# A chunked state-space scan feeding a GELU MLP: other queues for the decay rows, weight casts in pieces, and a new order of all steps

## The chip, the cores and the metric

The kernel runs on one core of a Trainium2 chip, in one launch. The metric is device time in microseconds (us) of that core. Five engines work beside one another and meet at semaphores: TensorE (PE, matmuls; its weight loads are shown as PEld), VectorE (DVE), ScalarE (ACT), GpSimd (POOL) and SyncE (SP, which here only issues DMAs). Each engine takes its own instructions strictly in the order in which they were emitted, so one that waits holds back all behind it.

## The reference, cut to what matters

Two stages, the second fed by the first. Stage one is a gated linear recurrence over 768 steps for 4 batches of 8 heads (head size 32, state size 16), written in chunks; stage two is a two-layer MLP with tanh GELU over the 3072 tokens, 256 wide, 2048 hidden.

```python
cum = np.cumsum(log(clip(a, 1e-06, 1.0)) of the chunk)
M = einsum('bhin,bhjn->bhij', C, B) * exp(cum_i - cum_j) * causal
y = M @ x + (C @ state) * exp(cum)
state = exp(sum) * state + sum_j B_j x_j * exp(cum_end - cum_j)
...
h = y.reshape(tokens, 256) @ w_in
out = gelu_tanh(h) @ w_out
```

Inputs and output are float32; the kernel multiplies in bf16.

## The kernel before, in words

The scan is done in chunks of 128 steps, 6 in a batch, 24 in all. A unit is one chunk (units 0 and 1) or two (units 2 to 12). The steps carry these names, in functions `f_<name>`:

- `clip`, `R`, `RT`, `recip` (DVE): suffix products of the decay, transposed, and their reciprocals. `pe`, `pp`, `pend`: the decay of whole chunks, brought to all rows by one matmul. POOL builds the constants that these need: `ident`, `bmask`, `tri`, `m8`; DVE builds `par` from `bmask` and `sel8`, `selp` from `ident`.
- `mul` (DVE): B times the suffix product, C times its reciprocal, one product each for a batch (`bc16`). `T` (PE): six transposes of such a product. `E`: copy of the result out of PSUM (`ch` for C, `bh` for B). `F` (or `F0` for batch 0): two copies of C masked by the parity of the head (`ce`). `N` (PE) and `bn`: B transposed back, and its copy.
- for a unit: `castx` (x to bf16), `G` (PE: C times B, into `gb`), `M` (DVE: the causal mask, `m`), `D` (PE: B times x, into `hp`), `S` and `SP` (DVE: the new state and its spread form), `Y` (PE: the unit's y, into `yb`), `yev` (ACT: y to `xm` in bf16).
- for the MLP: `s1` (PE: x times w_in, groups of four or eight matmuls into `hp` or `o_ps`), `gelu` (ACT, one for each group, into `gT`), `s2` (PE: four quarters of four matmuls for each chunk), `oev` (copy out of PSUM) and `store`. A group of s1 of units 0 and 1 needs one quarter of w_in, and a quarter of s2 one quarter of w_out.

From unit 4 on, `Y` of a unit, `D` and `G` of the next are emitted as one step. The weights come as float32: w_in in two loads of 1 MB (`wf`, each of two quarters), w_out in four of 512 KB, and are cast into `w_in_sb` [128, 2, 2048] and `w_out_sb` [128, 16, 256] on chip; the two "k halves" of a w_in quarter lie 2048 elements apart in a row. The casts, x among them, go through a helper (`copy`), so that they carry its line in the profile (L254 on POOL, L252 on ACT, L256 on DVE).

The order on each engine is not written by hand. Every step is a `Node` with an engine, a planned duration, the nodes that it needs, buffers that it takes from rotating pools, and a priority; `run_order` plays the plan through in time, takes at each moment the ready node with the lowest priority number on the engine that is free first, and emits the steps in that order. Loads are nodes of an engine "DMA", in the order in which they are added. Where TensorE would stand idle before the first `s1`, `idle` puts in filler matmuls on a zero tile `wz` (L747).

Before the plan starts, the decay rows `a` are fetched in four quarters:

```python
for q, eng in enumerate((nc.sync, nc.scalar, nc.scalar, nc.gpsimd)):
```

All other loads and the stores are issued from SP.

Of the kernel before, what the change touches and what calls it, by code (L numbers as in the profile page):

```python
# [14 lines left out]
class Node:  # L15


    def __init__(self, eng, dur, fn, deps=(), prio=0.0, done=0.0):
        self.eng, self.dur, self.fn, self.prio, self.done = eng, dur, fn, prio, done
        self.deps = [d for d in deps if d is not None]  # L20
        self.allocs = []
        self.after = 0.0
        self.start = self.end = None
# [7 lines left out]
def run_order(nodes, pools, hop=0.08, same=0.04, idle=None, wait=()):  # L31
# [6 lines left out]
    def est(n):  # L38
# [6 lines left out]
        for pool, _ in n.allocs:  # L45
            h = hist[pool]
            if len(h) >= pools[pool]:
                for d in h[-pools[pool]]:
                    if d.end is None:
                        return None  # L50
                    t = max(t, d.end + (same if d.eng == n.eng else hop))
        return t

    while todo:
# [25 lines left out]
        if idle is not None and eng == "PE":  # L80
            x = idle(free.get(eng, 0.0), t)
            if x is not None:
                order.append((free.get(eng, 0.0), x))
# [5 lines left out]
        order.append((t, n.fn))  # L89
    return order  # L90
# [3 lines left out]
def kernel(  # L94
# [24 lines left out]
    UNITS = [[0], [1]] + [[c, c + 1] for c in range(2, NCH, 2)]  # L119
    NU = len(UNITS)  # L120

# [32 lines left out]
    for q, eng in enumerate((nc.sync, nc.scalar, nc.scalar, nc.gpsimd)):  # L154
# [11 lines left out]
    for q in range(4):  # L166
        for t in (Q - 1, 2 * Q - 1) if q % 2 == 0 else (2 * Q - QS - 1, QS - 1):
# [6 lines left out]
    ident = const.tile([128, 128], BF16, name="ident")  # L174
    make_identity(nc, ident)
# [6 lines left out]
                            compare_op=ALU.is_ge, fill=0.0, base=N - 1, channel_multiplier=-1)  # L182
    tri = const.tile([128, Q], BF16, name="tri")
# [20 lines left out]
    par = const.tile([128, 2], FP32, name="par")  # L204
    bmp = bmask.rearrange("p (g e d) -> p e g d", g=4, e=2)
    for e in range(2):
        nc.vector.tensor_reduce(out=par[:, e:e + 1],
                                in_=bmp[:, e, :, 0:1].rearrange("p g o -> p (g o)"),
                                op=ALU.add, axis=mybir.AxisListType.X)
# [21 lines left out]
    def load_x(u):  # L231
        b, c = divmod(UNITS[u][0], CPB)
        XF[u] = ldx.tile([128, 2, H, D], FP32, name="x_t")
        for k in range(len(UNITS[u])):
            nc.sync.dma_start(out=XF[u][:, k], in_=x[b, :, (c + k) * Q:(c + k + 1) * Q, :]  # L235
                              .rearrange("h p d -> p h d"))

    wi = moe_w_in.rearrange("(k d) f -> d k f", d=128)
    wo = moe_w_out.rearrange("(q p k) m -> q p k m", p=128, k=4)

    def load_wi(h):
        WF[h] = wfp.tile([128, 2, d_ff // 2], FP32, name="wf")
        nc.sync.dma_start(out=WF[h], in_=wi[:, :, h * (d_ff // 2):(h + 1) * (d_ff // 2)])  # L243

    def load_wo(q):
        if q % 2 == 0:
            WF[("o", q // 2)] = wfp.tile([128, 8, d_model], FP32, name="wf")
        nc.sync.dma_start(out=WF[("o", q // 2)][:, 4 * (q % 2):4 * (q % 2) + 4], in_=wo[q])  # L248
# [9 lines left out]
    def f_wi(q, k0, k1, eng):  # L258
        copy(eng, w_in_sb[:, k0:k1, q * 512:(q + 1) * 512],
             WF[q // 2][:, k0:k1, 512 * (q % 2):512 * (q % 2) + 512])  # L260

    def f_wo(q, eng):
        copy(eng, w_out_sb[:, 4 * q:4 * q + 4], WF[("o", q // 2)][:, 4 * (q % 2):4 * (q % 2) + 4])
# [52 lines left out]
    def f_T(b, i):  # L316
        bc = U[b]["bc16"].rearrange("p i r h n -> p i r (h n)")
        if b == 0 and i == 1:
            T6_0[1] = pso.tile([128, 512], FP32, name="o_ps")[:, 0:S // 2].bitcast(BF16)
# [3 lines left out]
    def f_E(b, i, eng, p0=0, p1=128):  # L323
# [7 lines left out]
    def f_F0(e, eng, p0, p1):  # L331
# [27 lines left out]
    def f_bn(b, eng, c0=0, c1=CPB):  # L359
# [87 lines left out]
    def f_yev(u):  # L447
        n = len(UNITS[u])
        t0 = UNITS[u][0] * Q
        nc.scalar.activation(xm[:, :, t0:t0 + n * Q].rearrange("p w (c t) -> p c w t", c=n),  # L450
                             y4[:, 0:n], AF.Copy)
# [71 lines left out]

    MERGE = 4
# [3 lines left out]
    def add(eng, dur, fn, *args, deps=(), prio=0.0, done=None):  # L528
        n = Node(eng, dur, (lambda: fn(*args)), deps, prio,
                 (0.26 if eng == "PE" else 0.0) if done is None else done)  # L530
        n.name = f"{fn.__name__}{args}"
# [4 lines left out]
    TD = 1.85  # L536

    def none():
# [10 lines left out]

    an = load(TD + 0.3, none)  # L550
    an.done = 1.3

    def load_bc_n(b, *which):
        for i in which:
            bl[(b, i)] = load(1.6, load_bc, b, i)

    def load_x_n(*us):
        for u in us:
            xl[u] = load(0.87 * len(UNITS[u]), load_x, u)

    def load_w_n(*qs, o=False):
        for q in qs:
            if o:
                won_l[q] = load(1.5, load_wo, q)
            else:
                win_l[q] = load(2.5, load_wi, q)

    load_bc_n(0, 1, 0)
    load_w_n(0)
    load_x_n(0, 1)  # L570
    load_w_n(1)
    load_x_n(2)
    load_w_n(0, 1, 2, 3, o=True)
    load_x_n(3)
    for b in range(1, batch):
        load_bc_n(b, 1, 0)
        load_x_n(3 * b + 1, 3 * b + 2, 3 * b + 3)
    for q in range(4):
        wi_n[q] = [add(e, d, f_wi, q, k0, k1, e, deps=[win_l[q // 2]], prio=-9 + 0.1 * q)
                   for k0, k1, e, d in (((0, 1, "POOL", 0.53), (1, 2, "ACT", 0.56)) if q == 0 else  # L580
                                        ((0, 2, "POOL", 1.06),))]
        wo_n[q] = add("POOL", 1.06, f_wo, q, "POOL", deps=[won_l[q]], prio=20 + q)
# [201 lines left out]
```

## Time and profile before

| | us |
|---|---|
| median of 4 runs | 122.91 |
| lowest, highest | 122.55, 124.58 |
| the profiled execution's own time | 122.93 |
| its span, first to last instruction | 121.2 |
| TensorE busy | 111.1 (92%) |
| ACT busy | 75.0 (62%) |
| DVE busy | 63.0 (52%) |
| POOL busy | 20.5 (17%) |

A line of the profile names the source line, the engine, the operation, what it writes and reads, the shapes and the count. Busy time of TensorE is time with a matmul in flight, not time at its peak; the row PEclk gives the granted clock in tenths of full speed, the row DMA the mean busy share of the 16 DMA engines, both in 40 slices of the span. The chain of work that ended last follows the program back from its last instruction, at each step to what released it.

### The profile page before, as it was taken

The numbers are of one execution on the slowest core, as the hardware profiler recorded it, in microseconds if no ns is written. First come the engines' busy times: TensorE is split into PE (matmuls) and PEld (weight loads), VectorE is DVE, ScalarE is ACT, GpSimd is POOL, SyncE is SP. The second block draws the span as 40 slices with busy tenths as digits, with TensorE's granted clock in tenths as the row PEclk, the third lists the DMA queues.
The fourth block names the chain that finished last, engine by engine and source line by source line (L and its number), as shares of the span: only waits on it lengthen the run. The fifth ranks groups of instructions, "written<-read, shape, count | busy, mean of one in ns | idle before, by whom it ended". The sixth has DMA issues, their size and how long they took to land.

```text
span 121.2 us, 3425 instructions
## 1 busy us (share of the span) xinstructions
PE 111.1 (92%) x1470; PEld 98.3 (81%) x1470; DVE 63.0 (52%) x113; ACT 75.0 (62%) x145; POOL 20.5 (17%) x38
## 2 busy tenths in 40 slices
PE   4987549999999999999999999999999999999970
PEld 4964437988978888998889979798988999999950
DVE  5697932969539995908598527565563000000110
ACT  4029516695657675586675777775768766876210
POOL 5807086622212511202000000000000000000000
PEclk9999995999999999999999999999999999999998
DMA  2999989998899997811101101101110111101121
GB/s 61 297 334 219 246 265 381 220 231 151 153 289 164 185 275 123 149 47 49 43 0 43 47 2 43 46 3 49 43 43 0 49 43 46 43 6 43 43 87 46
DMA packets 38047, 13.96 MB, mean 115 GB/s; under 512 B 33824, under 2 KB 37008, under 8 KB 38032
## 3 DMA queue, kind: packets, MB, share of 16 engines
q1 hardware_dynamic: 37904, 13.67, 47.6%
q8 instruction: 11, 0.18, 0.7%
q10 hardware_dynamic: 96, 0.06, 0.2%
q14 instruction: 4, 0.03, 0.1%
q0 software_dynamic: 32, 0.02, 0.1%
HBM read 10.60 MB, written 3.15 MB: 113 GB/s over the span
## 4 chain that ended last, share of the span: by engine, by line
PE 66%; SPq 17%; DVE 7%; DMA 5%; issue 1%; DVEq 0%
PE o_ps L508 28%; PE hp L491 27%; SPq L248 6%; DMA bc_t<-in_B_dram 5%; SPq L243 4%; SPq L151 4%; SPq L235 3%; PE yb L508 3%; DVE ch L256 2%; PE gb L389 2%; PE yb L432 2%; PE yb L441 2%; DVE m L399 2%; PE gb L321 2%; DVE bc L310 2%
## 5 line engine op out<-in xcount | busy, mean ns | idle before, releaser
L499 ACT ACTIVATE gT<-hp 128x512 bf16<-128x512 f32 x94 | 52.0, 596 | 21.5 <-PE hp L491 21.4
L491 PE MATMUL hp<-xm,w_in_sb 128*128 128x256 bf16 (+1 forms) x400 | 51.4, 270 | 2.5 <-POOL w_in_sb L254 2.5
L508 PE MATMUL o_ps<-w_out_sb,gT 128*128 128x256 bf16 x352 | 47.0, 273 | 0.0
L491 PEld LDWEIGHTS <-w_in_sb 128*128 128x128 bf16 x416 | 42.5, 116 | 5.3 <-POOL w_in_sb L254 2.8
L508 PEld LDWEIGHTS <-gT 128*128 128x128 bf16 x384 | 37.1, 98 | 4.3 <-issue 0.4
L399 DVE TENSOR_TENSOR m<-gb,tri 128x1024 bf16<-128x1024 f32 (+1 forms) x25 | 29.0, 1175 | 0.6 <-PE gb L389 0.5
L517 DVE COPY o_sb<-o_ps 128x256 f32<-128x256 f32 x2 | 0.8, 425 | 25.2 <-PE o_ps L508 25.2
L254 POOL CAST x<-x_t 128x512 bf16<-128x512 f32 (+1 forms) x13 | 8.2, 638 | 25.3 <-DMA x_t<-in_x_dram 13.6
L460 DVE SCALAR_TENSOR_TENSOR s_new<-s_new,pend,hp 128x64 f32<-128x64 f32 x16 | 4.5, 281 | 15.0 <-PE hp L410 14.5
L515 ACT ACTIVATE o_sb<-o_ps 128x256 f32<-128x256 f32 x20 | 7.7, 386 | 4.4 <-ACT gT L499 2.7
L467 DVE SCALAR_TENSOR_TENSOR sp_new<-s_new,pend,bmask 128x256 bf16<-128x256 f32 x20 | 10.3, 525 | 0.0
L450 ACT ACTIVATE xm<-yb 128x512 bf16<-128x512 f32 (+1 forms) x13 | 7.4, 569 | 3.6 <-PE hp L410 3.0
L747 PE MATMUL yb<-wz 128*128 128x128 bf16 x64 | 6.7, 294 | 1.6 <-DVE warm L161 1.6
L747 PEld LDWEIGHTS <-wz 128*128 128x128 bf16 x68 | 6.5, 138 | 1.6 <-DVE warm L161 1.6
L441 PE MATMUL yb<-m,x 128*32 128x128 bf16 x192 | 6.2, 220 | 0.6 <-POOL x L254 0.6
L389 PE MATMUL gb<-ce,bh 32*128 32x256 bf16 x96 | 5.0, 283 | 0.5 <-DVE m L399 0.4
L458 DVE COPY s_new<-hp 128x64 f32<-128x64 f32 x4 | 0.9, 223 | 8.6 <-PE hp L410 8.6
L432 PE MATMUL yb<-ce,sp_new 128*32 128x128 bf16 x160 | 5.3, 221 | 0.0
L338 ACT ACTIVATE ce<-o_ps,par 128x258 bf16<-128x258 bf16 (+1 forms) x4 | 2.1, 581 | 5.1 <-PE o_ps L321 5.1
L441 PEld LDWEIGHTS <-x 128*32 128x32 bf16 x192 | 3.7, 96 | 1.4 <-POOL x L254 0.8
L321 PEld LDWEIGHTS <-bc 128*128 128x128 bf16 x48 | 3.2, 97 | 2.0 <-issue 1.0
L254 POOL CAST w_in_sb<-wf 128x1024 bf16<-128x1024 f32 (+1 forms) x4 | 3.6, 933 | 6.7 <-DMA wf<-in_moe_w_in_dram 6.7
(61 smaller groups left out, 62.4 us busy)
## 6 DMA issues: line engine op xcount, KB each, us to landing
x_t<-in_x_dram SPq DMA_DIRECT2D x24, 128.0 KB, 4.4
out_dram<-o_sb SPq DMA_DIRECT2D x24, 128.0 KB, 1.7
wf<-in_moe_w_in_dram SPq DMA_DIRECT2D x2, 1024.0 KB, 8.6
wf<-in_moe_w_out_dram SPq DMA_DIRECT2D x4, 512.0 KB, 5.6
bc_t<-in_C_dram SPq DMA_DIRECT2D x4, 384.0 KB, 4.6
bc_t<-in_B_dram SPq DMA_DIRECT2D x4, 384.0 KB, 5.1
a_t<-in_a_dram SPq DMA_DIRECT2D x1, 32.0 KB, 1.7
a_t<-in_a_dram ACTq DMA_DIRECT2D x1, 32.0 KB, 2.4
```

Of the source, the lines that this page charges most:

```text
L254: nc.gpsimd.tensor_copy(out=o, in_=i)
L389: nc.tensor.matmul(out=gb[:, g, 256 * k:256 * k + 256], lhsT=bh_of(gc)[32 * g:32 * g + 32], rhs=ce_of(gc)[32 * g:32 * g + 32], start=True, ...
L399: nc.vector.tensor_tensor(out=MT[gc][:, g0:g1], in0=gb[:, g0:g1, 256 * (k + half(u)):256 * (k + half(u)) + 256] .rearrange("p g (e t) -> p ...
L432: nc.tensor.matmul(out=y4[32 * j:32 * j + 32, k, w], lhsT=sp[:, 32 * h:32 * h + 32], rhs=ce_of(gc)[:, h % 2], start=first(j), stop=False, ...
L441: nc.tensor.matmul(out=y4[32 * j:32 * j + 32, k, w], lhsT=X16[u][:, k, 32 * h:32 * h + 32], rhs=m[:, h // 2, h % 2, :], start=first(j), st ...
L450: nc.scalar.activation(xm[:, :, t0:t0 + n * Q].rearrange("p w (c t) -> p c w t", c=n), y4[:, 0:n], AF.Copy)
L467: nc.vector.scalar_tensor_tensor(out=sp_new.rearrange("p (g d) -> p g d", g=4), in0=state[("s", gc)].rearrange("p (o d) -> p o d", o=1).to ...
L491: nc.tensor.matmul(out=hp[:, j * nt:(j + 1) * nt], lhsT=w_in_sb[:, kc].rearrange("p (q m k) -> p q k m", m=128, k=4)[:, fi // 4, fi % 4], ...
L499: nc.scalar.activation(gts[u][:, i * per:(i + 1) * per, 0:nt], hps.pop((u, i)).rearrange("p (j t) -> p j t", j=per), AF.Gelu_apprx_tanh)
L508: nc.tensor.matmul(out=ops[gc], lhsT=gts[u][:, fi, tt * Q:(tt + 1) * Q], rhs=w_out_sb[:, fi, :], start=(fi == 0), stop=(fi == NF - 1), ski ...
L515: nc.scalar.activation(o_sb, ops.pop(gc), AF.Copy)
L747: nc.tensor.matmul(out=(gb[:, 3] if g_next else yb)[:, 384:512], lhsT=wz[:, 0:128], rhs=wz[:, 0:128], start=True, stop=True)
```

## The change

Seven things differ. What the built programs hold is said beside them.

1. The last quarter of the decay rows is fetched from SP instead of POOL. SP so issues two decay rows ahead of C and B of batch 0.
2. On POOL `bmask` is built first, then `ident`; on DVE `par` comes ahead of `sel8` and `selp`.
3. A weight quarter is cast in two pieces of 128x512 (each k half by itself), 16 in all. Twelve are on POOL, two on ACT (second halves of w_in quarters 0 and 1) and two on DVE (first half of w_in quarter 3, second half of w_out quarter 3). On POOL, after the second w_in load, the order is second half of quarter 3, second half of quarter 2, first half of quarter 2, then x of unit 2, then w_out.
4. All rotating buffers are counted in the plan, each step's buffers one by one.
5. x is loaded by chunks, chunk 1 before chunk 0. B of batch 2 comes ahead of C and ahead of x of chunk 8; the first three stores stand among the loads.
6. Filler matmuls may take as their right operand what a named step has just written (`ac`, `r_t`, `rt`, x, `m`, `w_in_sb`), so that they wait for it. There are 105 of them, 68 before.
7. Priorities and some engines come from a table, `TUNE` and `ENG`; durations in the plan are set anew.

The order that results on TensorE up to the first transposes of batch 1, as far as it differs (in words: G 0 is `G` of unit 0, s1 0.2 is the third s1 group of unit 0, s2 0/1 the second quarter of chunk 0; at [w_in] stands the first step that needs the second half of w_in):

```
before: Y 0, D 0, D 1, G 2, s1 0.0, s1 0.1, Y 1, [w_in] s1 0.2, s1 1.0, s1 0.3, s1 1.1, D 2, G 3, s1 1.2, s1 1.3, Y 2,
        s2 0/0, 0/1, s1 2.0, 2.1, s2 0/2, s1 2.2, 2.3, s2 0/3, s1 2.4, D 3, s2 1/0, 1/1, s1 2.5, 2.6, T 1 (C), Y 3,
        s1 2.7, T 1 (B), s2 1/2, ...
after:  D 1, Y 0, D 0, G 2, s1 0.0, Y 1, s1 0.1, s1 1.0, s1 1.1, [w_in] s1 0.2, D 2, G 3, s1 0.3, s1 1.2, Y 2,
        s2 0/0, s1 1.3, s2 0/1, s1 2.0, 2.1, s2 0/2, s1 2.2, s2 0/3, s1 2.3, 2.4, s2 1/0, D 3, s2 1/1, s1 2.5,
        s2 1/2, 1/3, s1 2.6, 2.7, Y 3, T 1 (C), T 1 (B), s2 2/0, ...
```

On DVE two more `recip` stand before and after the two products of batch 0, `pe` stands before `RT`, and `bn` of batch 0, one masked C and `bn` of batch 1 are new; `bh` of batches 0 and 1 moves to ACT. In batch 1 both products precede the copies; in batch 2 the two transposes follow each other, and B's product stands ahead of the states and masks of unit 4. The diff, cut:

```diff
-        for pool, _ in n.allocs:
-            h = hist[pool]
-            if len(h) >= pools[pool]:
-                for d in h[-pools[pool]]:
+        for i, (pool, _) in enumerate(n.allocs):
+            h, j = hist[pool], sum(p == pool for p, _ in n.allocs[:i])
+            if len(h) + j >= pools[pool]:
+                for d in h[len(h) + j - pools[pool]]:
...
+    for n in nodes:
+        if n.emit_after is not None:
+            at = {r[2]: i for i, r in enumerate(order) if r[2] is not None}
+            i, j = at[n], at[n.emit_after]
+            if i < j and not any(r[2] is not None and r[2].eng == n.eng for r in order[i + 1:j]):
+                order.insert(j, order.pop(i))
...
-    for q, eng in enumerate((nc.sync, nc.scalar, nc.scalar, nc.gpsimd)):
+    for q, eng in enumerate((nc.sync, nc.scalar, nc.scalar, nc.sync)):
...
-    def f_wi(q, k0, k1, eng):
-        copy(eng, w_in_sb[:, k0:k1, q * 512:(q + 1) * 512],
-             WF[q // 2][:, k0:k1, 512 * (q % 2):512 * (q % 2) + 512])
-
-    def f_wo(q, eng):
-        copy(eng, w_out_sb[:, 4 * q:4 * q + 4], WF[("o", q // 2)][:, 4 * (q % 2):4 * (q % 2) + 4])
+    def f_wi(q, k, eng):
+        copy(eng, w_in_sb[:, k, q * 512:(q + 1) * 512],
+             WF["i", q // 2][:, k, 512 * (q % 2):512 * (q % 2) + 512])
+
+    def f_wo(q, k, eng):
+        copy(eng, w_out_sb[:, 4 * q + 2 * k:4 * q + 2 * k + 2].rearrange("p k m -> p (k m)"),
+             WF["o", q // 2][:, q % 2, 512 * k:512 * k + 512])
...
+        name = "_".join([fn.__name__[2:]] + [str(v) for v in args])
+        opts = eng if isinstance(eng, dict) else None
+        if opts:
+            eng = ENG.get(name, next(iter(opts)))
+            dur = opts[eng]
+            args = args + (eng,)
+        n = Node(eng, dur, (lambda: fn(*args)), deps, TUNE.get(name, prio),
...
+    FIRST = "C0 B0 i0 x0 x1 i1 x2 x3 o0 o1 o2 o3 x4 x5"
+    for item in FIRST.split() + [f"{t}{b}" if t in "CB" else f"x{CPB * b + int(t)}"
+                                 for b in range(1, batch) for t in "CB012345"]:
...
+    cast = {"POOL": 0.6, "ACT": 0.62, "DVE": 0.45}
     for q in range(4):
-        wi_n[q] = [add(e, d, f_wi, q, k0, k1, e, deps=[win_l[q // 2]], prio=-9 + 0.1 * q)
-                   for k0, k1, e, d in (((0, 1, "POOL", 0.53), (1, 2, "ACT", 0.56)) if q == 0 else
-                                        ((0, 2, "POOL", 1.06),))]
-        wo_n[q] = add("POOL", 1.06, f_wo, q, "POOL", deps=[won_l[q]], prio=20 + q)
+        wi_n[q] = [add(cast, 0, f_wi, q, k, deps=[win_l[q // 2]], prio=-9 + 0.1 * q) for k in range(2)]
+        wo_n[q] = [add(cast, 0, f_wo, q, k, deps=[won_l[q]], prio=20 + q) for k in range(2)]
...
+    for u, cs in enumerate(UNITS):
+        xcn[u].takes("x16", Yn[u], Dn[u])
+        min((xl[c] for c in cs), key=lambda n: (TUNE.get(n.name, n.prio))).takes("ldx", xcn[u])
...
+    paced = {cl: lambda: ac[:, 0:128].bitcast(BF16)[:, 1::2],
+             R_: lambda: r_t[:, 0:128].bitcast(BF16)[:, 1::2],
+             RT_: lambda: rt.rearrange("p r b -> p (r b)")[:, 0:128].bitcast(BF16)[:, 1::2],
+             xcn[0]: lambda: X16[0][:, 0, 0:128]}
...
-    pools = {"hp": 2, "o": 1, "gram": 2, "yb": 1, "wf": 4, "ob": 6}
+    pools = {"x16": 6, "ldx": NU, "m": 4, "s": 4, "sp": 4, "hp": 2, "o": 1, "gram": 2, "yb": 1, "wf": 3, "ob": 6}
```

## The prediction

> **What bounds the kernel now.** I read the page's first two blocks, then the chain of work that ended last, then what TensorE waited for, then the timeline of the first 30 us, and last the windows of one clock period each.
>
> ```profile
> span 121.2 us, 3425 instructions
> PE 111.1 (92%) x1470; PEld 98.3 (81%) x1470; DVE 63.0 (52%) x113; ACT 75.0 (62%) x145; POOL 20.5 (17%) x38
> PE   4987549999999999999999999999999999999970
> PEclk9999995999999999999999999999999999999998
> DMA  2999989998899997811101101101110111101121
> ...
> PE 66%; SPq 17%; DVE 7%; DMA 5%; issue 1%; DVEq 0%
> ```
>
> TensorE is full from the seventh slice (18 us) on; later only less or faster work could save much, and the change alters neither. Idle TensorE, the one 5 of its clock and most of the DMA load fall in the first seven slices. The chain says the same: SPq and DMA (loads) until 28 us, TensorE after that. What TensorE waited for, then the timeline (start, length; the bracket is the idle time before), then the one load in the chain:
>
> ```profile
> PE hp L491 <- POOL w_in_sb L254: 2.5, 2, 1.7
> ```
>
> ```profile
> 14.08 0.29 PE L441 MATMUL yb<-m,x 128*32 128x128 bf16 x8
> 16.11 0.25 PE L491 MATMUL hp<-xm,w_in_sb 128*128 128x128 bf16 x1 [1.74 <-POOL w_in_sb L254]
> 17.10 1.35 PE L491 MATMUL hp<-xm,w_in_sb 128*128 128x128 bf16 x15 [0.74 <-POOL w_in_sb L254]
> ...
> 15.01 2.03 POOL L254 CAST w_in_sb<-wf 128x1024 bf16<-128x1024 f32 x2 [3.09 <-DMA wf<-in_moe_w_in_dram]
> 17.54 0.62 POOL L254 CAST x<-x_t 128x512 bf16<-128x512 f32 x1 [0.50 <-DMA x_t<-in_x_dram]
> 22.80 1.04 POOL L254 CAST w_out_sb<-wf 128x1024 bf16<-128x1024 f32 x1 [0.46 <-DMA wf<-in_moe_w_out_dram]
> ```
>
> ```profile
> 22.34 6.03 DMA bc_t<-in_B_dram
> ```
>
> TensorE stands 1.74 + 0.74 us for the second half of w_in, which lands at 15.0. It then needs both quarters: after one matmul at 16.11 it waits again until the POOL cast of the last quarter ends at 17.04. That second wait is needless: a cast of both k halves covers, taken as one interval of the row, addresses that the other quarter's second half also holds. POOL waits for a load before each of these casts, so weights and x are bound by the loads; B of batch 1 lands at 28.37. The windows (the clock halves at 17.64 and is back at 21.05, so I cut by that length):
>
> ```profile
> core 0: us, PE busy (x), PEclk, DMA share, GB/s
> 10.82:14.23 3.41, 2.33 (x60) 1.00 0.95 281
> 14.23:17.64 3.41, 0.93 (x23) 1.00 0.93 229
> 17.64:21.05 3.41, 3.41 (x43) 0.50 1.01 380
> ```
>
> After a window 27% busy the clock is halved for exactly one window of 3.41 us, all of it work: 1.7 us lost. So 2.5 us of idleness and 1.7 us of slow clock, 4.2 us, are what there is to win.
>
> **The change part by part.**
>
> *Decay rows.* Rows went out on SP, ACT twice and POOL; landing took 1.7, 1.8, 2.4 and 3.3 us, so POOL's (issued at 1.32) came last at 4.62 and DVE's clip started at 4.68. After: two on SP, all landed at about 3.65 (ACT's second, 1.25 + 2.4). POOL loses an issue of 0.65, SP gains one: its issues follow each other by 0.44, so every later load starts 0.44 later. The Trainium skill's "DMA: Bandwidth & Descriptors" (section "Issuing engines are not separate DMA queues") speaks against the gain: another issuer saves only the issue time. By the rule the rows come no sooner and SP pays 0.44; by the row they come 1 us sooner. I take the row, but the gain stops on DVE: clip is queued behind par, sel8 and selp, which wait for POOL's masks (about 0.65 sooner than now) and end near 3.9; the two pe steps now stand before the transpose RT and wait for POOL's last m8 select (6.05 now, about 5.4 then), and a second reciprocal (0.45) stands before the first product. So the first product starts at 5.4 + 0.18 + 0.52 + 2 x 0.45 = 7.0, against 6.78: nothing won. I charge the full 0.44 on all loads (DMA share near 1.0 from 2.75 us leaves no room to catch up); the other end is 0.
>
> *First chunks.* DVE gets two more reciprocals, one masked C (0.43) and both bn copies (0.3 + 0.4, estimates under ACT's 0.40 and 0.62) and loses one bh copy (0.43), so the masks m end at about 13.5 instead of 12.56 and the first s1 group starts near 13.9, not 12.95. It costs nothing: what covers it is the wait for w_in. Fillers (105 matmuls, 68 before) wait in TensorE's order for casts and DVE steps; all of those end before the steps that follow need them. If the clock is still slow at 6 us, the 26 fillers behind RT take 2.8 us and push the first transpose from about 8.0 to 8.5-9; the cover (the wait at D of unit 2, below) holds that too.
>
> *Casts in pieces.* Each piece is its own address range, so the false wait goes; four s1 groups (two of chunk 1 now ahead of the third of chunk 0) run before the second w_in half. On POOL the order there is quarter 3's second half, then quarter 2's two: 15.45 + 3 x 0.61 = 17.3, so the third s1 group of chunk 0 starts at 17.3, hardly later than today's 17.1 in spite of the late load. Then D of unit 2 stands in TensorE's order, and waits for x: 17.54 + 0.44 landing + 0.62 cast = 18.6. Behind it wait G, s1 and s2. From there, with a group each 0.44 (the start-to-start of groups at full clock):
> D and G to 19.15; two s1 groups 20.05; Y of unit 2 (0.56) 20.6; first s2 quarter 21.05 (its w_out pieces 19.17 + 2 x 0.61 = 20.4); s1 21.5; second quarter, POOL done 21.66, 21.9; two s1 22.8; third quarter, POOL 22.92, 23.15; s1 23.6; fourth quarter, w_out landing 22.80 + 0.44, POOL 0.61 beside DVE, 23.9 to 24.1. Today the same work plus one s1 group ends at 26.03: 26.03 - (24.1 + 0.44) = 1.5 us ahead, with 0.85 + 0.8 us of waits left for loads.
> The DVE casts (0.25 to 0.66; the upper end is ACT's row for 128x512) and ACT's two lie beside those waits; DVE's of w_in is not late before 18.9, of w_out not before 23.9.
>
> *Clock.* In the window 14.23 to 17.64 TensorE would be busy some 2.2 us of 3.41 (64%), against 27% today and 68% in the window before it, which kept the clock. "TensorE: Matmul & The Clock Gate" (section "What's actually happening") lets the clock fall after an idle window of about 3.4 us, and the section "Why this matters for your kernels" warns of gaps over 3 us. This trace has no gap over 1.74 us and fell all the same, so the measurement decides: the mean over a window counts. By the rule the clock is safe (121.3); by the row it is near the safe end, and if it falls, 121.7 (below).
>
> *Batch 1.* From 24.1, 4.8 us of matmuls precede the second transpose, with some 0.3 of turnovers: TensorE is there at 29.2 but B lands at 28.37 + 0.44 and its product takes 0.96: start 29.85, end 30.2, where today it ends at 30.61 with 0.87 us (two s2 quarters) less done: 0.41 + 0.87 = 1.3 us ahead. The load takes back 0.2. The bh copy goes to ACT (about 0.82, like bn's 0.81), bn to DVE; 1.3 us of groups stand before N and cover the first.
>
> *Later.* The next wait for a transpose (45.06 to 45.37) goes, since both halves of batch 2 are transposed at once long after their products: 0.3. The third (66.6) stays, and at unit 4's Y the two orders have done the same sum of work. B of batch 2 is loaded before x of chunk 8, and its product stands on DVE ahead of M of unit 4; SP, in order, holds x of chunk 7, this B and x of chunk 8 behind the first store, that is until about 24.8. By the rows it lands near 32.5, DVE wants it at 32.7: no cost, but no cover beyond 0.7 us.
>
> *Sum:* 1.3 + 0.3 = 1.6 us. The profiled execution took 122.93 with its 121.2 span, the median is 122.91: so 121.3. About 0.3% is what a measurement of this kernel can tell.
>
> **The rivals.**
> One half-clock window (17.64 to 21.05): the work from 18.6 takes twice as long up to 21.05, the fourth s2 quarter ends near 25.0, but the wait at the transpose (0.6) swallows most: 0.4 us of gain lost, 121.7. For: 64% is below 68%. Against: it is far from 27%. Chance 0.15.
> Two windows, the slower end: if the windows' phase or the 1.6 us of waits between 16.5 and 18.6 keep the clock at half from 17.64 to 24.46, the fourth quarter ends at 26.8, the transpose at 32.3 instead of 30.2, the kernel at 123.4. It decides at about 5 us of half clock; beyond that each us costs half a us. For: the clock ran at half for the 51 fillers today (5.62 us, 0.11 each) with TensorE full, so it is slow to rise. Against: today it rose after one full window. Chance 0.13, with kin of the same sign.
> Late loads: the new places of stores and B on SP cost DVE and TensorE a us, 122.5 (0.14): the seventeen waits of SP for o_sb speak for it, the DMA backlog until 35 us against.
> More won: loads shifted by less than 0.44, no turnovers: 120.5 (0.08).
> That it doesn't do what it says is ruled out by the order of the built program.
>
> **How the numbers follow.** The forecast has 0.50, 121.3 with its own range 120.7 to 121.8 (loads 0 to 0.44 later, late handoffs 0.4). Faster by over 0.3% (below 122.54): 0.50 + 0.15 + 0.08 + 0.05 of the late loads = 0.78; within 0.3%: 0.07 of the late loads; slower: 0.13 and the last 0.02 of them. The range 120.5 to 122.8 leaves out the two-window case and the far end of the best.
>
> **What would show it.** Right: PEclk without a 5 in the seventh slice, no second wait for w_in, TensorE waiting for x at D of unit 2 until about 18.6, the fourth s2 quarter near 24, the batch 1 transposes near 30. Wrong: half clock after 17 us, loads not 0.4 later, TensorE waiting for DVE at Y of unit 4, or a wait after 45 us that is not there today.

## The result, and the profile after

The changed kernel takes 122.46 us (median of 36 runs, 121.31 to 123.83), the kernel before, run beside it, 123.19 us (57 runs): ratio 0.994, 95% interval 0.9923 to 0.9958, or 0.7 us less (0.5 to 0.95). The forecast was 1.6 us less. The profiled execution took 122.29 us. Ratios, and the means by granted clock below, leave out runs more than 1.5% above the fastest of their kernel.

The page after: PEclk is full in all slices, TensorE has no slice under 9 from the twelfth (33 us) to the last but one, and the chain has less SPq but now a DMA of w_out in it.

```profile
span 120.5 us, 3506 instructions
PE 112.2 (93%) x1507; PEld 99.5 (83%) x1507; DVE 64.2 (53%) x120; ACT 75.5 (63%) x143; POOL 19.8 (16%) x41
PE   4996979989899999999999999999999999999990
PEclk9999999999999999999999999999999999999999
DMA  1997999999999799761101101101110111011121
...
PE 74%; SPq 13%; DMA 6%; DVE 3%; issue 1%; POOL 1%; ACT 1%; DVEq 0%
```

What TensorE waited for (us in total, times, longest). The wait for w_in fell from 2.5 to 0.8 us; two new ones are there, for w_out and for the copy `bh`, and the two for `ch` (0.3) are gone.

```profile
PE o_ps L783 <- ACT ce L350: 1.1, 1, 1.1
PE hp L502 <- POOL w_in_sb L264: 0.8, 1, 0.8
PE gb L368 <- ACT bh L262: 0.6, 1, 0.6
PE o_ps L519 <- POOL w_out_sb L264: 0.6, 2, 0.4
```

The windows of one clock period, cut as before (columns: busy us and count of PE, PEld, DVE, ACT and POOL, then PEclk, DMA share, GB/s). The middle one is 84% busy where the forecast had 64%: four s1 groups, Y of unit 1 and the end of G of unit 2, all real work. No window is slow.

```profile
core 0: us, PE busy (x) PEld busy (x) DVE busy (x) ACT busy (x) POOL busy (x), PEclk, DMA share, GB/s
10.82:14.23 3.41, 2.31 (x49) 1.68 (x46) 2.89 (x6) 2.16 (x5) 1.63 (x4) 1.00 0.87 254
14.23:17.64 3.41, 2.86 (x56) 2.20 (x48) 3.41 (x6) 2.50 (x5) 1.75 (x3) 1.00 1.02 257
17.64:21.05 3.41, 2.96 (x75) 2.41 (x76) 2.56 (x5) 1.90 (x5) 3.06 (x6) 1.00 0.98 297
```

The timeline of the places that the forecast named: the three POOL pieces of w_in and the s1 group behind them, x of unit 2, the fourth s2 quarter, and batch 1.

```profile
15.88 2.04 POOL L264 CAST w_in_sb<-wf 128x512 bf16<-128x512 f32 x3 [3.44 <-DMA wf<-in_moe_w_in_dram]
17.88 0.80 POOL L264 CAST x<-x_t 128x512 bf16<-128x512 f32 x1
17.99 0.64 PE L502 MATMUL hp<-xm,w_in_sb 128*128 128x128 bf16 x8 [0.82 <-POOL w_in_sb L264]
...
24.84 0.60 PE L519 MATMUL o_ps<-w_out_sb,gT 128*128 128x256 bf16 x4 [0.37 <-POOL w_out_sb L264]
...
30.11 0.84 PE L333 MATMUL gb<-ident,bc 128*128 128x128 bf16 x12
...
30.99 0.96 DVE L266 COPY ch<-gb 128x768 bf16<-128x768 bf16 x1 [1.24 <-PE gb L333]
...
31.98 0.81 ACT L262 ACTIVATE bh<-gb 128x768 bf16<-128x768 bf16 x1 [1.16 <-DVE ch L266]
...
32.84 0.51 PE L368 MATMUL gb<-ident,bh 128*128 128x128 bf16 x6 [0.58 <-ACT bh L262]
```

The last three rows are the surprise: `bh` on ACT waits for `ch` on DVE, though it needs nothing of it, and TensorE stands before N.

To see where time came from I added up TensorE's real work in each trace. Each matmul (fillers left out) counts as much as it takes from start to start at full clock: 0.109 us for 256 columns of s1 and s2, 0.056 for a transpose, 0.042, 0.020 and 0.014 for one of G, D and Y. All kernels hold 98.42 us of it. The time less the work begun by then is TensorE's lost time; two kernels at the same lost time are level, whatever their order. The columns are two traces of each kernel (the second ones come from runs e1 and a0 below):

```
at us     before 1  before 2   after 1  after 2
 18         14.19     14.63     14.03    14.03
 24         15.86     15.32     14.99    15.10
 28         16.07     15.64     15.75    15.75
 30         16.41     16.41     15.87    15.90
 32         16.66     16.98     15.89    16.00
 36         16.77     17.10     16.77    16.88
 48         17.32     17.41     17.13    17.13
110         18.78     18.89     18.57    18.67
last matmul
ends at    117.40    117.51    117.22   117.28
span       121.21    121.33    120.46   120.52
```

On the mean the change is 0.9 us ahead at 32 us, 0.1 ahead at 36, 0.2 at the end of TensorE. Of the 0.88 us that the first trace of the changed kernel loses from 32 to 36 us, 0.74 are the wait at N (0.85 us from the start of the last s1 matmul, 31.99, to N at 32.84, where 0.11 is usual). From the last matmul to the end of the span the kernel before takes 3.81 and 3.82 us, the changed one 3.24. So of 0.8 us between the spans, 0.2 is TensorE's and 0.6 lies behind the last matmul, where no step of the forecast looked.

### The profile page after: what moved, and what is told of

It reads as the page before. It is cut to its first block, busy times and chain, and to the rows that moved or that the text cites. A ratio compares the mean times of both kernels' runs of the same rounds, so it can differ in the third digit from the quotient of the medians.

```text
span 120.5 us, 3506 instructions
## 1 busy us (share of the span) xinstructions
PE 112.2 (93%) x1507; PEld 99.5 (83%) x1507; DVE 64.2 (53%) x120; ACT 75.5 (63%) x143; POOL 19.8 (16%) x41
## 4 chain that ended last, share of the span: by engine, by line
PE 74%; SPq 13%; DMA 6%; DVE 3%; issue 1%; POOL 1%; ACT 1%; DVEq 0%
PE hp L502 30%; PE o_ps L519 30%; DMA wf<-in_moe_w_out_dram 6%; SPq L252 4%; SPq L258 4%; SPq L244 3%; PE yb L519 3%; PE gb L401 2%; PE yb L444 2%; PE yb L453 2%; PE gb L333 2%; DVE ch L266 2%; PE gb L368 1%; SPq L159 1%; POOL w_out_sb L264 1%
## 5 line engine op out<-in xcount | busy, mean ns | idle before, releaser
L510 ACT ACTIVATE gT<-hp 128x512 bf16<-128x512 f32 x94 | 52.7, 596 | 18.8 <-PE hp L502 18.5
L519 PE MATMUL o_ps<-w_out_sb,gT 128*128 128x256 bf16 x352 | 47.6, 273 | 0.6 <-POOL w_out_sb L264 0.6
L502 PEld LDWEIGHTS <-w_in_sb 128*128 128x128 bf16 x416 | 41.9, 114 | 3.9 <-issue 1.6
L528 DVE COPY o_sb<-o_ps 128x256 f32<-128x256 f32 x3 | 1.3, 425 | 26.3 <-PE o_ps L519 26.3
L783 PEld LDWEIGHTS <-wz 128*128 128x128 bf16 x105 | 8.8, 124 | 2.9 <-DVE warm L169 1.6
L478 DVE SCALAR_TENSOR_TENSOR sp_new<-s_new,pend,bmask 128x256 bf16<-128x256 f32 x20 | 9.8, 492 | 0.1
L783 PE MATMUL yb<-wz 128*128 128x128 bf16 x35 | 3.8, 291 | 1.6 <-DVE warm L169 1.6
L266 DVE COPY ch<-gb 128x768 bf16<-128x768 bf16 x3 | 2.9, 958 | 4.4 <-PE gb L333 4.4
L264 POOL CAST w_out_sb<-wf 128x512 bf16<-128x512 f32 x7 | 4.6, 680 | 1.5 <-DMA wf<-in_moe_w_out_dram 1.5
L264 POOL CAST w_in_sb<-wf 128x512 bf16<-128x512 f32 x5 | 3.2, 675 | 9.1 <-DMA wf<-in_moe_w_in_dram 9.1
```

Source lines behind the costliest of these rows:

```text
L264: nc.gpsimd.tensor_copy(out=o, in_=i)
L478: nc.vector.scalar_tensor_tensor(out=sp_new.rearrange("p (g d) -> p g d", g=4), in0=state[("s", gc)].rearrange("p (o d) -> p o d", o=1).to ...
L502: nc.tensor.matmul(out=hp[:, j * nt:(j + 1) * nt], lhsT=w_in_sb[:, kc].rearrange("p (q m k) -> p q k m", m=128, k=4)[:, fi // 4, fi % 4], ...
L510: nc.scalar.activation(gts[u][:, i * per:(i + 1) * per, 0:nt], hps.pop((u, i)).rearrange("p (j t) -> p j t", j=per), AF.Gelu_apprx_tanh)
L519: nc.tensor.matmul(out=ops[gc], lhsT=gts[u][:, fi, tt * Q:(tt + 1) * Q], rhs=w_out_sb[:, fi, :], start=(fi == 0), stop=(fi == NF - 1), ski ...
L783: nc.tensor.matmul(out=bank[:, 384:384 + w], lhsT=wz[:, 0:128], rhs=r, start=True, stop=True)
```

## The experiments

Ratios are to the kernel before, run beside them on the same chip, with 95% intervals. "Tail" is the time from the end of the last matmul to the end of the span, "lost" TensorE's lost time at 36 us in the trace.

| run | kernel | ratio | lost | tail |
|---|---|---|---|---|
| e1_before | before, again | 1.0002 [0.9968, 1.0035] | 17.10 | 3.82 |
| b3_before_fill | before, fillers in the gap | 0.9971 [0.9937, 1.0005] | 16.67 | 3.81 |
| b4_before_pieces | before, w_in in pieces | 0.9938 [0.9899, 0.9978] | 16.77 | 3.31 |
| c4_before_hp | before, B of batch 1 in hp | 1.0011 [0.9979, 1.0044] | 16.88 | 3.81 |
| c3_before_pieces_hp | before, both | 0.9943 [0.9902, 0.9985] | 16.45 | 3.32 |
| b5_before_row_sp | before, row on SP | 1.0025 [0.9999, 1.005] | 17.21 | 3.60 |
| a0_after | changed, again | 0.9948 [0.9922, 0.9975] | 16.88 | 3.25 |
| a1_row_act | changed, row on ACT | 1.0038 [1.0009, 1.0067] | 18.36 | 3.25 |
| a2_row_pool | changed, row on POOL | 0.996 [0.9934, 0.9986] | 16.88 | 3.31 |
| b1_c_act | changed, C on ACT | 1.0095 [1.0057, 1.0133] | 19.01 | 3.25 |
| c2_sp_dummy | changed, one more SP load | 0.9993 [0.9957, 1.0029] | 17.43 | 3.33 |
| d2_q2_first | changed, quarter 2 first | 0.995 [0.9921, 0.9978] | 17.65 | 3.24 |
| a3_bh_hp | changed, B of batch 1 in hp | 0.9869 [0.9824, 0.9914] | 16.56 | 3.25 |
| c1_bh_hp | the same | 0.9939 [0.991, 0.9968] | 16.12 | 3.25 |
| b2_c_act_bh_hp | hp, C on ACT | 1.0032 [0.9996, 1.0067] | 18.09 | 3.25 |
| d4_pool_bh_hp | hp, row on POOL | 0.992 [0.9879, 0.9961] | 16.23 | 3.31 |
| d1_q2_bh_hp | hp, quarter 2 first | 0.9893 [0.9853, 0.9933] | 16.34 | 3.25 |
| e2_q2_bh_hp | the same | 0.9892 [0.9848, 0.9936] | 16.99 | 3.25 |

**The wait of `bh` for `ch`.** Both copies read `gb`, `bh` its part 0 and `ch` its part 2 of four; nothing of `ch` enters `bh`. Yet in all seven traces of the changed kernel without the edit below ACT's `bh` waits 1.16 us and starts when DVE's `ch` has ended. The order of the engines can be the other one: in batch 0 ACT's `ce` starts at 8.75 and takes 0.48, and DVE's `ce`, from the same `o_ps`, starts at 9.26. The edit lets the transposes of B write another tile:

```diff
     def f_T(b, i):
+        if b == 1 and i == 0:
+            state["tb"] = psh.tile([128, 512], FP32, name="hp")[:, 0:S // 2].bitcast(BF16)
...
-            nc.tensor.transpose(out=(T6 if b else T6_0)[i][...]
+            nc.tensor.transpose(out=t6_of(b, i)[...]
```

> The changed kernel, but the six transposes of B of batch 1 write a buffer of hp instead of gb, so that the bh copy on ACT reads another PSUM tile than the ch copy on DVE and does not wait for it. Theory 2 (this wait is where the gain went): bh starts at about 30.85 instead of 31.98, TensorE does not stand 0.58 us before N, and the kernel takes 0.4 to 0.6 us less than the changed kernel. Theory 1 (loads decide) or a DVE chain behind (ce, bn, the masks of unit 4 end when they ended): 0 to 0.2 us less, and the wait turns up again at Y of unit 4 (39.1).

> The changed kernel with B of batch 1 transposed into a buffer of hp, as once before (121.41 us, six runs): more runs and a second trace. Theory (the one chain B lands, product, transpose, ch copy, bh copy, N holds TensorE at 32.8 us whatever was won earlier): ratio to the kernel before 0.984 to 0.991, no wait before N of batch 1, lost time of TensorE at 36 us 0.3 to 0.7 us under the changed kernel's. If the six runs were luck: 0.993 or more.

The timeline of c1 (start, length): `bh` starts 0.33 us after `ch`, beside it, and N at 32.22 without a wait.

```profile
30.39 0.50 PE L338 MATMUL hp<-ident,bc 128*128 128x128 bf16 x6
30.59 0.96 DVE L266 COPY ch<-gb 128x768 bf16<-128x768 bf16 x1 [0.48 <-PE gb L338]
30.92 0.81 ACT L262 ACTIVATE bh<-hp 128x768 bf16<-128x768 bf16 x1 [0.17 <-PE hp L338]
...
32.22 0.50 PE L373 MATMUL gb<-ident,bh 128*128 128x128 bf16 x6
```

The wait is gone in all six traces with the edit in the changed kernel: from 32 to 36 us they lose 0.0 to 0.3 us, the seven without it 0.7 to 0.9. The two runs a3 and c1 disagree on its worth (their intervals barely meet). Weighted by the number of runs, the changed kernel with the edit (a3, c1, d1, d4, e2) is at 0.991 and without it (the first measurement, a0, a2, d2) at 0.995: about 0.5 us, near the 0.58 us of the wait. The pairs that ran side by side on one chip and differ in this edit alone say somewhat more: a3 against a0 0.008, d1 against d2 and b2 against b1 0.006 each, 0.7 to 1.0 us.

**The row's queue.** One word of the row's line is changed, or one load is added or moved.

```diff
-    for q, eng in enumerate((nc.sync, nc.scalar, nc.scalar, nc.sync)):
+    for q, eng in enumerate((nc.sync, nc.scalar, nc.scalar, nc.scalar)):   # a1; nc.gpsimd in a2
...
+    nc.sync.dma_start(out=spare_a, in_=...)    # c2: 24 KB that nobody reads, behind the rows
...
+    load_bc(0, 1, nc.scalar)                   # b1: C of batch 0 from ACT, behind its rows
```

> The changed kernel as it is, run beside its variants: the base from which each of them is read, and a second trace that tells how far one trace can be trusted. Both theories: ratio to the kernel before 0.992 to 0.996; fourth s2 quarter of chunk 0 at 24.6 to 25.0 us, second transposes of batch 1 at 30 to 30.8, TensorE waits 0.5 to 0.6 us for the bh copy (L262). If the wait for bh or the lateness of the loads is a matter of this one execution, they differ here by 0.5 us or more.

> The changed kernel with the fourth decay row on ACT instead of SP, all else as it is. Theory 1 (SP's second row makes the loads late, and late loads cost the missing 0.9 us): every load from C of batch 0 on is issued 0.44 us sooner, weights land 0.5 to 1.0 us sooner, the fourth s2 quarter of chunk 0 starts at 24.0 instead of 24.84, and the kernel takes 0.4 to 0.7 us less than the changed kernel. Theory 2 (the bh copy of batch 1, which waits for the ch copy, swallows what stands ahead of it): the loads come sooner, but N of batch 1 starts at most 0.3 us sooner; under 0.3 us gained. Theory 3 (the loads are late by the order of x or by the DMA engines, not by the row): landings move by under 0.2 us.

> The changed kernel with the fourth decay row on POOL again, as in the kernel before. It undoes this one part. Theory 1 (late loads): loads 0.44 us or more sooner, while clip, the scan and the first products start up to 1 us later; net 0 to 0.5 us faster. If the first chain decided, it is 0.3 to 0.9 us slower. Theory 2 (bh copy): same within 0.3 us.

> The changed kernel, with C of batch 0 issued from ACT behind its two decay rows, so that SP's two rows no longer push every later load back by one issue: rows early and weights early together. Theory 1 (the gain was lost to late weights): the w_in casts on POOL start about 0.7 us sooner (9.8 and 15.2 instead of 10.5 and 15.9), the fourth s2 quarter of chunk 0 starts near 24.1 instead of 24.9, and the kernel takes 0.3 to 0.7 us less than the changed kernel (median 122.72 there). Theory 2 (the bh copy's wait swallows it): weights sooner, N of batch 1 still near 32.6 to 32.9, under 0.3 us less. Against both: a load issued from ACT at 1.7 us can come late (the fourth decay row, third on ACT, landed only at 6.2); if C does, the first product is late by 0.5 to 2 us and the kernel is 0.3 to 1.2 us slower.

> The changed kernel with both edits: C of batch 0 from ACT, and B of batch 1 transposed into a buffer of hp so that the bh copy does not wait for the ch copy. If the two costs are one behind the other (late weights, then the wait), the gains add: about 120.7 to 121.2 us against 121.4 with the second alone. If only the wait counts: as with the second alone, 121.3 to 121.6. It is also the version that should beat both kernels.

> The changed kernel with one more 24 KB load of a decay row (into a tile that nobody reads) on SP, behind the two rows: a second dose of what moving the row did to the loads, with the decay rows as early as in the changed kernel. If late loads cost what they are late: every load 0.44 us later or a little more, and the kernel 0.4 to 0.7 us slower than the changed kernel (122.46 to 122.72). If the lateness is hidden (by TensorE's other work, or by the bh copy's wait): within 0.25 us of it.

> The changed kernel with the hp edit and the fourth decay row on POOL as in the kernel before. With the wait in place the row's queue made no difference that could be measured (0.996 against 0.995). If that wait hid a difference, it shows now: row on SP better by 0.3 us or more (this one at 0.994 or above) where the late first chain costs more than late weights, or POOL better (0.988 or below) where late weights cost more. If the two sides of the trade are equal in themselves: 0.990 to 0.994, as with the hp edit alone.

> The kernel before with the fourth decay row on SP: this part of the change alone, in the old order. Loads 0.44 to 0.9 us later, clip about 1 us sooner (3.6 to 3.8 instead of 4.7 to 4.9). Late-weights theory: there TensorE waits for w_in at 14.4 us whatever the first chain does, so the early chain is worth nothing and the late loads cost 0.3 to 0.7 us: ratio 1.002 to 1.006. If the first chain is worth what the loads cost: 0.998 to 1.002.

Times in us in the traces: means of the eight that have two rows and all other loads on SP, of the six of the kernel before and its variants that have one row on POOL, and c2 alone.

```
                                row on SP   row on POOL   one more on SP
w_in half 1, POOL's first cast    10.50        9.78           11.24
w_in half 2, POOL's first cast    15.84       15.14           16.38
clip                               3.48        4.71            3.43
```

The columns also differ in the order of the kernels. Within the new order the w_in loads are 0.7 us later with the row on SP (seven traces against a2 and d4); within the old one, where b5 is the only such trace, 0.5. So one SP issue (0.44 us long) makes them 0.5 to 0.7 us late, and brings clip at least 1.2 us sooner. A second such issue (c2) costs 0.5 to 0.7 us of lateness again, and 0.005 of the ratio, 0.6 us (its interval just touches those of the changed kernel): late loads seem to be paid nearly in full. The trace of c2 has a half-clock window at 12.6 us, but its five runs with a granted clock of 0.994 or more are no faster (123.19 on the mean) than the other seven (123.13). But the row back on POOL (a2) gains nothing: its loads come early, its clip at 5.03, and 0.996 cannot be told from 0.995, with the wait for `bh` or without it (d4, 0.992, against 0.991). The two sides of the trade are about equal in the new order. In the old one (b5) clip comes at 3.39 and the loads late, and TensorE waits longer for x; there it costs some 0.3 us, 0.5 if its shorter tail is taken off:

```profile
12.23 0.40 PE L441 MATMUL yb<-m,x 128*32 128x128 bf16 x8 [2.21 <-POOL x L254]
```

The late loads need not be all of that cost. The trace of b5 has two half-clock windows (from 12.13 and from 18.96 us), and the granted clock was under 0.978 in ten of its twelve runs, against four of the 26 of the kernel before beside it; b5 does not tell the two apart.

My attempts to have both, row and loads early, failed. The third load on ACT comes late beside SP's large ones. In a1 the row, issued at 1.72, held clip until 6.30; the DVE row of the trace:

```profile
6.30 0.29 DVE L278 TENSOR_SCALAR ac<-a_t 128x256 f32<-128x256 f32 x1 [2.93 <-DMA a_t<-in_a_dram]
```

In b1 it is C that comes late; the issues (KB, us to landing) of b1 first, then of a0:

```profile
bc_t<-in_C_dram ACTq DMA_DIRECT2D x1, 384.0 KB, 8.2
```

```profile
bc_t<-in_C_dram SPq DMA_DIRECT2D x1, 384.0 KB, 3.7
```

Both theories were wrong on b1; the warning at the end of its expectation came true, and more than it said: the first product starts at 10.02, 3.8 us late, and the kernel loses 1.9 us against the changed one. A half-clock window from 11.97 us, after a window that was 23% busy, may be part of it.

**Why a gain ahead of 30 us did not count in the kernel before.** Three edits of the kernel before win time early: fillers in the gap (which hold the clock), w_in in pieces, and the hp edit.

```diff
         hps[(u, i)] = hp
+        if (u, i) == (0, 2):                              # b3
+            for _ in range(23):
+                nc.tensor.matmul(out=yb[:, 384:512], lhsT=wz[:, 0:128], rhs=wz[:, 0:128], ...)
...
-        copy(eng, w_in_sb[:, k0:k1, ...], WF[q // 2][:, k0:k1, ...])
+        for k in range(k0, k1):                           # b4 and c3
+            copy(eng, w_in_sb[:, k, ...], WF[q // 2][:, k, ...])
```

> The kernel before, with 23 filler matmuls (yb<-wz) ahead of the third s1 group of chunk 0, in the gap where TensorE waits for the second half of w_in. Nothing else differs. Clock theory (what the change won is the half-clock window at 17.6 us): the window goes, the granted clock is 1.0 in nearly all runs, and the kernel takes 0.4 to 0.5 us less than before, as its own runs without such a window do (span 121.25 against 121.7). If the 1.7 us lost in the window lay on the path, 1.2 us or more; if the wait at the transposes of batch 1 swallows all of it, under 0.2 us.

> The kernel before, with each w_in quarter cast by one instruction for each k half, in the same order on POOL; nothing else. The third s1 group of chunk 0 no longer waits for the last quarter's cast (0.74 us). Theory A (the false wait cost its length): 0.5 us less or more. Theory B (behind it TensorE waits for x of unit 2 and w_out anyway, and POOL's four instructions end when its two did): 0 to 0.25 us less.

> The kernel before with two edits: w_in casts one k half at a time, and B of batch 1 transposed into a buffer of hp, so that these transposes do not wait for the ch copy on DVE. In the kernel before with the first edit alone TensorE stood 1.21 us at these transposes and had lost no less time at 32 us than without it. If that wait swallows what is won ahead of it: it goes or falls under 0.4 us, N of batch 1 starts near 31.5 instead of 32.4, and the kernel takes 0.5 to 1.0 us less than with the casts alone (122.45), about 121.5 to 122.0. If the bh copy on DVE (behind ch) is then waited for instead: 0 to 0.3 us less.

> The kernel before with the second of these edits alone: B of batch 1 transposed into a buffer of hp. There the wait at these transposes was 0.17 us in the profiled execution. If it costs only its length: 0.1 to 0.3 us less than before. If in most executions it is longer than in the profiled one (those with no or a short half-clock window reach it earlier): 0.3 to 0.6 us less.

> The kernel before, unchanged: a second trace of it. Its first trace had one half-clock window and a last store that landed 3.8 us after the end of TensorE, where the other traces have 3.2 to 3.3. If that trace was like most: TensorE's lost time at 44 us 16.6 to 17.1 and its end at 117.2 to 117.6. If it was a fast one (which would explain why the medians differ by 0.7 us and the traces' ends of TensorE by 0.2): 17.2 or more, end 117.8 or later, last store 3.2 to 3.3 after it.

b4's lost time is 14.55 at 24 us, 1.3 under the first trace of before, and 16.41 at 30, exactly as there. The transposes of B of batch 1 in the first trace of before, in b4, then in e1:

```profile
30.28 0.49 PE L321 MATMUL gb<-ident,bc 128*128 128x128 bf16 x6 [0.17 <-DVE ch L256]
```

```profile
30.32 0.49 PE L322 MATMUL gb<-ident,bc 128*128 128x128 bf16 x6 [1.21 <-DVE ch L256]
```

```profile
30.58 0.49 PE L321 MATMUL gb<-ident,bc 128*128 128x128 bf16 x6 [0.82 <-DVE ch L256]
```

These transposes begin at 30.28, 30.58, 30.18 and 30.32 in before, e1, b3 and b4, while the transposes of C ahead of them vary from 27.48 to 28.49. B lands near 28.4, its product takes 0.96, and the `ch` copy, 0.95, follows on DVE; the transposes wait for that. The wait of 0.17 us in the first trace was short only because TensorE was late. It was a floor, and in the traces it also swallowed the half-clock window: b3, whose fillers hold the clock at full from 5.3 us on, has lost as much at 30 us as the first trace, and its last matmul ends with it at 117.40. (e1, at full clock from 5.5 us, ends no sooner either, but its second half of w_in came 0.6 us later, 15.65 against 15.01.)

Over many runs the window was not free. b3 is at 0.997, 0.4 us less, with an interval that reaches 1. And of 156 runs of the kernel before that stand beside the variants, the 41 with a granted clock of 0.994 or more took 122.94 us on the mean, the 104 from there down to 0.978, about one window, 123.22, and the 11 below that 123.49. So a first window goes with some 0.3 us, and more of them with 0.6. These runs differ by chance and not by an edit, so that the window is the cause is likely but not shown.

The hp edit removes this wait too: in c3 TensorE has lost 0.3 us less than in b4 at 36 us, which the two ratios do not show; alone (c4) it shows nothing. Both traces ran at half clock for 6.83 us (from 12.86 and 13.05), and no run of c4 had the full clock, so what the edit is worth in the old order stays open.

**The order on POOL.** Both halves of w_in quarter 2 ahead of quarter 3's second half:

```diff
-'wi_2_0': -10.7994, 'wi_2_1': -11.7451,
+'wi_2_0': -11.79, 'wi_2_1': -11.78,
```

> The changed kernel with quarter 2 ahead of quarter 3 on POOL, nothing else. If the bh copy's wait swallows what is won ahead of it: TensorE is earlier at 22 us by 0.3 to 0.6 and the wait before N of batch 1 grows by as much as is left of it; ratio to the kernel before as the changed kernel's, 0.993 to 0.996. If not: 0.990 to 0.992.

> The changed kernel with B of batch 1 in a buffer of hp (no wait of the bh copy for the ch copy) and, on POOL, both halves of w_in quarter 2 ahead of quarter 3's second half. Theory (TensorE stands 0.8 to 1.3 us for quarter 2, which POOL finishes last of three): the third s1 group of chunk 0 starts at about 17.2 instead of 18.0, lost time of TensorE at 22 us falls by 0.3 to 0.6, and with no wait left at N of batch 1 the kernel takes 0.2 to 0.5 us less than with the hp edit alone (ratio to the kernel before 0.987 and 0.994 there), about 0.988. If loads (x of unit 2, w_out) set the front whatever POOL's order is: the same as with the hp edit alone, 0.991 to 0.994.

> The changed kernel with the hp edit and w_in quarter 2 first on POOL, as once before (0.9893 of the kernel before, six runs): more runs. If both edits help: 0.987 to 0.991. If the order on POOL is worth nothing and the hp edit 0.4 to 0.6 us: 0.990 to 0.993.

TensorE no longer waits for w_in; it waits 0.7 to 0.8 us for x of unit 2 instead, as in d1:

```profile
18.51 0.24 PE L427 MATMUL hp<-x,bn 128*32 128x64 bf16 x8 [0.72 <-POOL x L264]
```

So the wait only moves, to x and in d2 and e2 also to w_out (1.4 and 1.3 us in total, 0.6 in the changed kernel), and d2 is where the changed kernel is. d1 and e2, the same kernel with the hp edit, are at 0.989 both times: 1.3 us under the kernel before and some 0.6 us under the changed one. What the order adds to the hp edit these runs do not separate from nothing.

**The tail.** It was not planned as an experiment, but all traces hold it. After the last store has landed, the engines meet at semaphores, and POOL, in between, clears the semaphores. POOL's last seven records, as us after the last matmul (length in ns), with the number of its records in the trace:

```
before   73  WAIT 2.59, SIGNAL 2.67, DRAIN 3.10 (233), CLEAR 3.37 (139), DRAIN 3.54 (40), WAIT 3.62, SIGNAL 3.71
b5       72  WAIT 2.58, SIGNAL 2.66, DRAIN 2.74 (82),  CLEAR 3.19 (96),  DRAIN 3.32 (52), WAIT 3.41, SIGNAL 3.50
b4       76  WAIT 2.59, SIGNAL 2.67, DRAIN 2.75 (93),  CLEAR 2.87 (139), DRAIN 3.05 (40), WAIT 3.13, SIGNAL 3.21
after    75  WAIT 2.58, SIGNAL 2.66, DRAIN 2.74 (82),  CLEAR 2.85 (96),  DRAIN 2.98 (34), WAIT 3.06, SIGNAL 3.14
```

In before a gap of 0.41 us stands ahead of the DRAIN, which is POOL's 69th record. In b5, with one record less, a gap of 0.37 us stands ahead of the CLEAR, which is its 69th there. With 75 records the 69th is the first of these seven, the WAIT, and with 76 it is the one ahead of them: there POOL waits for the store anyway, and the seven have no gap. All twenty traces fit: those with 73 records (before, e1, b3, c4) have 3.81 to 3.83 us, the one with 72 has 3.60, the fifteen with 75 or 76 have 3.24 to 3.33. It looks like the crossing into the next piece of POOL's code, and the packets of the instruction queues speak for it. From 117 us to the end before has one (queue, kind, packets, MB, share), a0 none:

```profile
q14 instruction: 1, 0.01, 0.3%
```

It holds 8 KB. The five traces with a gap have such a packet behind the last matmul, the fifteen others have one at 55 to 59 us instead, at most 1.5 us behind POOL's last cast. It starts 0.68 to 0.72 us after POOL's 69th record wherever that record is not the WAIT: at 121.20 after 120.51 in before, at 121.88 after 121.19 in b5, at 55.80 after 55.10 in b4. So a fetch goes with that record. But it starts after the gap, and what fills the gap itself is not shown. The Trainium skill's "Runtime: NRT & Kernel Launch" (section "Instruction fetch mechanics") calls the cost of crossing a block boundary mostly hidden; if this is such a crossing, it is hidden at 75 records and costs 0.4 us and more at 73. The kernel before with one more instruction on POOL and no other change was not tried.

## Why the prediction was right or wrong

The sign was right, and the size was wrong by more than half; most of what was measured came from a place that the prediction did not name. That the range (120.5 to 122.8) held the time is luck: with the tail of the kernel before it would have been 123.0.

The step that failed is the cover at N of batch 1: "The bh copy goes to ACT ...; 1.3 us of groups stand before N and cover the first". The forecast carried 1.3 us across it to the end. In its place the copy waited for `ch`, TensorE stood, and of 0.9 us won by 32 us 0.1 was left at 36. Second, the lateness of the loads was mis-sized: 0.44 us was charged, and 0.5 to 0.7 came for w_in, 1.1 for the last w_out in the trace.

- *Clock.* Right that no slow window remains in the trace, and in all but four of the runs the granted clock was 0.99 or more. The 1.7 us counted among "what there is to win" were mis-sized: in the traces the wait at the transposes of batch 1 swallowed them (b3), and over the runs of the kernel before a window goes with 0.3 us. The worry that 64% of busy time is near the safe end did not come to a test, as the window was 84% busy.
- *The needless wait for w_in.* Right that it goes (b4). Worth little in the kernel before for the same reason: b4's 0.76 us are 0.50 us of tail and some 0.2 at TensorE's end, so that its Theory A had the number by luck.
- *Decay rows.* The charge of 0.44 us on the loads, "the other end is 0", was mis-sized: the second half of w_in was cast from 15.88 instead of 15.45, and the three casts took 2.04 instead of 1.83, so the third s1 group started at 17.99 instead of 17.3; the last w_out load came 1.1 us later than before (23.9 against 22.80), so the fourth s2 quarter started at 24.84. "Nothing won" on the first product was wrong the other way: it started at 6.25, 0.5 sooner than before, not at 7.0. That the skill's rule, as the prediction cites it, and the row disagreed was settled for the row, but only in this place: rows issued ahead of C come early, and what comes behind SP's large loads comes late from ACT and POOL alike (a1, a2, b1; POOL's row in a2 took 3.7 us, SP's second in a0 1.9).
- *The 1.5 us at the fourth quarter.* The sum let the quarter end at 24.1, a quarter of a us behind POOL's cast (22.80 + 0.44 + 0.61 = 23.85). But the second half is DVE's, so all four matmuls wait for POOL's piece and end at 24.3, which leaves 1.3. Measured: 24.84 + 0.88 = 25.72, 0.3 us ahead of 26.03; the difference is the late load (0.7 beyond the charge) and a cast of 0.87 instead of 0.61. And 26.03 stands behind a half-clock window: in e1, without one, the same point is 25.54, ahead of the changed kernel.
- *Batch 1.* Forecast 1.3 us ahead at the transposes; measured 0.9 on the mean of the traces at 32 us. Then came the cover that failed. The groups were there, but the copy waited 1.16 us for `ch`, TensorE 0.58 us for the copy, and 0.8 of the 0.9 us were gone at 36 us. The order of emission was read, the waits of the built program were not.
- *Later.* The wait at the first transposes of batch 2 went, as forecast, but between 36 and 110 us only some 0.1 us of the 0.3 came of it.
- *The end.* Nothing was said of it. 0.57 us of the measured 0.73 lie there.

Of the rivals "Late loads" came nearest in time (122.5), for other reasons than its own: the stores and B of batch 2 cost nothing that the traces show.

## What to carry to other kernels

A short wait at a handoff may be a floor: ask when what it waits for is ready, and whether anything won ahead of it can pass; here fillers, casts in pieces and a trace at full clock all met transposes that began at 30.2 to 30.6 us. When a copy moves to another engine, look at the waits of the built program, not at the data it needs: two readers of one PSUM tile can be put one behind the other. And take the end of TensorE apart from the end of the span before a difference of half a us is given to the change.

## What the runs showed of the hardware that I had not expected

- The number of POOL's instructions went with 0.57 us at the end of the program (3.81 us of tail at 73 records, 3.24 at 75): POOL's 69th record starts some 0.4 us late where it falls into the closing handshake.
- One load of 24 KB ahead of the queue, 0.44 us of issue, made loads of 1 MB land 0.5 to 0.7 us later (b5, c2 and the rows above).
- A 384 KB load that SP lands in 3.7 us took 8.2 us when ACT issued it at the same 1.7 us, behind two rows of its own and beside SP's loads of B, w_in and x.
- The clock's windows, cut at each trace's own changes of clock: up to 40 us it fell to half eight times, after six windows that were 23 to 49% busy and two that were 67% (c3, c4). Twenty-three windows of 50 to 69% kept it. So under half is where it fell in these traces, but the share of one window does not settle it above.
